# A scheduled kernel of a long convolution beside a gated feed-forward layer: the order of all engines from a per-operation table, b1 by one load and two column-tile transposes, 20 instead of 38 filler matmuls

## The chip, the cores and the metric

One core of one Trainium2 chip. The metric is the device time of one launch in microseconds (us), given as the median of several runs; the lowest and the highest run are in brackets. The profile's span is about 1.8 us shorter than the time of the same execution, because the time includes the start and end around the instructions. PE is TensorE's matmul, PEld its weight load, DVE is VectorE, ACT is ScalarE, POOL is GpSimd, SP is SyncE, which here mostly issues DMAs. A run counts as slow when it is over 1.5% above the fastest run of its kernel.

Ratios are the mean time of one kernel's fast runs over that of the kernel before in the same rounds on the same chip, so they are not quite the ratio of the medians that I quote.

## The reference

Shapes: sequence 2048, width D = 640, hidden width F = 1728, all bfloat16. Cut to what matters:

```python
x  = A_q                                   # 1 x 2048 x 640
xn = _layernorm(x)
# branch A: short convolution of k (4 taps), times v, then a convolution of length 2048 by FFT
k_shift = sum_t k_pad[:, t:t+S, :] * shift_k[:, 3-t]
kv = k_shift * v
y  = irfft(rfft(kv, 4096) * rfft(ssm_k, 4096))[:2048] + kv * ssm_D
s  = xn * y
# branch B: feed-forward layer with gelu, then silu as a gate
g  = silu(gelu(xn @ w1 + b1) @ w2 + b2)
# ... the output joins x, s and g
```

The kernel does the FFT as matmuls in stages, through scratch tensors in DRAM: a first stage for the filter's keys (scrK) and for kv (scrU), a small forward stage in tiles of 64 x 32, a product, an inverse in tiles of 32 x 64 (stored to scrC), and a last stage.

## The kernel before

The kernel is a list of operations. A planner (`Plan`) places each on an engine at a planned start, with a cost for each operation and a priority; the instructions are then emitted in the order of the planned starts. The psf and psa buffers are the kernel's PSUM buffers, where matmuls write: two psf of 512 columns and three psa of twice 512. The parts that the change and the argument touch:

```python
MODE_SWITCH = 0.095
# in Plan.schedule(): one pair of numbers for each kind of operation
for k, os in kinds.items():
    a, b = self.due[k]
    for i, o in enumerate(os):
        o.prio = -(a + (b - a) * i / max(1, len(os) - 1))
# ... list scheduling by the key (start, -prio, cost) ...

for i in range(38):                        # fillers, to raise TensorE's clock
    ps = Buf(pool=psf)
    op("PE", 0.22, lambda e, ps=ps: nc.tensor.matmul(out=ps.v[:, :], lhsT=hT_t[0][:, FT - 2, 0:P],
                          rhs=hT_t[0][:, FT - 2, :], start=True, stop=True), reads=[warm_b], writes=[ps], kind="warm")
# ... b1: memset, two loads on ScalarE's queue, one transpose, one copy
op("PE", 0.1, lambda e, ps=ps: nc.tensor.transpose(out=ps.v.bitcast(BF16)[:, 0:FT], in_=b1_r[:], identity=...))
op("DVE", 0.08, lambda e, ps=ps: nc.vector.tensor_copy(out=b1_f[:], in_=ps.v.bitcast(BF16)[:, 0:FT]))
# ... ffn1: one FF1 group of five matmuls of 512 columns into one of two psf banks, then gelu on ScalarE
for t in range(DT):
    nc.tensor.matmul(out=o, lhsT=w1_sb[:, t, ft*P:(ft+1)*P], rhs=xnT_b[c].v[:, :, t, :], start=(t == 0), stop=(t == DT-1))
# ... the small forward stage: eight matmuls in tiles of 64 x 32
def fwd(ps, src, z):
    for t in range(4):
        for r in range(2):
            nc.tensor.matmul(out=ps.v[t*32:t*32+32, r, 0:H], lhsT=F2m[r*Q:r*Q+Q, z*32:z*32+32],
                             rhs=src[r*Q:r*Q+Q, t, :], start=True, stop=True)
# ... middle(h, g): reload a group of the scratch into uin, forward stage, product, inverse, store to scrC
op("SP", 0.46, lambda e: nc.sync.dma_start(out=uin.v, in_=by_group(scrU[h], g)), ...)
```

Of the kernel before, what the change touches and what calls it, by code (L numbers as in the profile page):

```python
# [15 lines left out]
P = 128  # L16
# [50 lines left out]
TABLE_LOAD = 1.28  # L67
MODE_SWITCH = 0.095

class Plan:  # L70
# [42 lines left out]
    def schedule(self):  # L113
# [6 lines left out]
        for o in ops:  # L120
            for d in o.after:
                follow[d].append(o)
        kinds = {}
        for o in ops:
            kinds.setdefault(o.kind, []).append(o)
        for k, os in kinds.items():
            a, b = self.due[k]
            for i, o in enumerate(os):
                o.prio = -(a + (b - a) * i / max(1, len(os) - 1))
        for o in ops:  # L130
# [9 lines left out]
        while ready:  # L140
            best = None
            for o in ready:
                est, slots, ok = o.est, [], True
                for b in o.allocs:
                    cand = None
                    if b.pool.fifo and b.seq != b.pool.next:
                        ok = False
                        break
                    for s in b.pool.slots:
                        if any(s is c for c in slots) or any(u.done is None for h in s[1] for u in h.users):  # L150
                            continue
                        t = max([u.done for h in s[1] for u in h.users], default=0.0)
                        if cand is None or t < cand[0]:
                            cand = (t, s)
                    if cand is None:
                        ok = False
                        break
                    est = max(est, cand[0])
                    slots.append(cand[1])
                if not ok:  # L160
                    continue
                for e in o.engs:
                    t = max(est, free[e])
                    c = o.cost[e]
                    p = o.prio
                    if e == "ACT" and o.table is not None and o.table != table:
                        c += TABLE_LOAD
                        p -= self.due["switch"][0]
                    if e == "PE" and o.mode != mode:
                        c += MODE_SWITCH  # L170
                        p -= self.due["mode"][0]
                    if e != o.engs[0]:
                        wait, less = self.due["dve" if e == "DVE" else "pool"]
                        if max(est, free[o.engs[0]]) <= t + wait:
                            continue
                        p -= less
                    key = (t, -p, c)
                    if best is None or key < best[0]:
                        best = (key, o, e, t, c, slots)
# [33 lines left out]

DUE = {
    "b1": (-2658.69, -12.83), "cab0": (8557.17, 6667.77), "cab1": (-1486.18, -152.64), "cst0": (-305.42, 2707.06),
    "cst1": (-2821.97, -4792.38), "dve": (0.47, 30.2), "f1_0": (-871.05, 1734.66), "f1_1": (1301.71, 4641.74),
    "f1_2": (1114.17, 1732.61), "f1_3": (2717.88, 2832.21), "f1k0": (-526.64, -1917.59), "f1k1": (-45.43, 1009.63),
    "f1u0": (-4387.08, -5449.77), "f1u1": (-871.6, -2537.05), "f2_0": (-101.73, 568.69), "f2_1": (55.74, -1410.81),
    "f2_2": (2347.64, 580.24), "f2_3": (1367.74, 4253.7), "f2k0": (-4800.76, 938.43), "f2k1": (1474.47, -1695.6),
    "f2u0": (1087.17, -104.99), "f2u1": (-2201.6, -388.99), "fin0": (3005.36, 3026.91), "fin1": (4769.18, 4253.19),  # L220
    "first": (-4156.08, -3068.36), "gtab": (-2228.31, -2211.96), "halo1": (3569.33, 2410.81),
    "i10": (-236.08, -1811.7), "i11": (-1708.64, -1347.6), "i20": (2541.11, 1052.7), "i21": (2701.42, 3183.93),
    "kin0": (-593.69, 758.66), "kin1": (1951.88, -1170.69), "kt": (-677.48, -1093.47), "kv0": (-3727.38, -6497.24),
    "kv1": (818.93, -2911.39), "ln0": (-2934.3, -4187.58), "ln1": (-6791.26, -5326.47), "ln2": (1941.49, 937),
    "ln3": (896.12, -1662.13), "load1": (-2919.94, -4066.71), "load10": (1978.17, 919.81),
    "load11": (-2440.26, -3260.22), "load12": (4122.04, 8470.58), "load13": (7611.05, 3845.84),
    "load14": (3186.96, 908.54), "load15": (4188.27, 3598.3), "load16": (-1111.28, -467.99),
    "load17": (3134.69, 3049.36), "load18": (376.5, 3182.36), "load19": (1982.23, 428.93),
    "load2": (-5152.92, -6327.1), "load20": (5478.92, 7432.46), "load21": (-2345.4, 472.84),
    "load22": (-3453.91, -1273.89), "load23": (3030.08, 3625.43), "load24": (-2431.86, -3878.73),  # L230
    "load3": (-4653.66, -5026.1), "load4": (-4049.51, -2679.33), "load5": (-3127.18, -2370.67),
    "load6": (-1295.43, -2222.83), "load7": (-3086.77, -1734.57), "load8": (-486.48, 2101.2),
    "load9": (1995.94, 1552.87), "mode": (197.93, 0), "ones1": (-1676.37, -2952), "pool": (7.25, -13.8),
    "prod0": (69.2, -3781.34), "prod1": (2713.4, -508.43), "small": (-2624, 2474.77), "switch": (23.42, 0),
    "uin0": (-5019.36, -4445.98), "uin1": (-4066.58, -3058.07), "warm": (-9990.03, -8766.04),
    "wexp": (462.86, 314.56), "wtab": (-4840.89, -4511.51), "xt0": (-2587.15, -3103.92), "xt1": (191.84, -3623.5),
    "xt2": (1912.14, 2825.82), "xt3": (-3593.86, -3830.63),
}

@with_exitstack  # L240
def kernel(
# [47 lines left out]
    I1m = sb.tile([P, 3, Q], BF16, name="I1m")  # L289
    b1_r = sb.tile([FT, P], BF16, name="b1_r")  # L290
    b1_f = sb.tile([P, FT], F32, name="b1_f")
# [27 lines left out]

    plan = Plan(DUE)  # L320
    op = plan.op
# [6 lines left out]

    EV = (0.585, 0.735)
    psf = Pool(psf_t, fifo=False)  # L330
    psa = Pool(psa_t, fifo=False)
# [26 lines left out]
    op("DVE", 0.45, c0, writes=[bias_b, ones_b, mh_b], kind="first")  # L358
    op("DVE", 0.14, lambda e: nc.vector.memset(b1_r[:], 0.0), writes=[b1r_b], kind="first")

    warm_b = Buf()
    op("DVE", 0.2, lambda e: nc.vector.memset(hT_t[0][:, FT - 2, :], 0.0), writes=[warm_b], kind="first")
    for i in range(38):
        ps = Buf(pool=psf)
        op("PE", 0.22, lambda e, ps=ps: nc.tensor.matmul(out=ps.v[:, :], lhsT=hT_t[0][:, FT - 2, 0:P], rhs=hT_t[0][:, FT - 2, :],  # L365
                                                         start=True, stop=True),
           reads=[warm_b], writes=[ps], kind="warm")
# [8 lines left out]
    def load_rows(e):  # L376
        nc.scalar.dma_start(out=sk_row[0:1, :], in_=A_shift_k.rearrange("d j -> (d j)").rearrange("(o f) -> o f", o=1))
        nc.scalar.dma_start(out=dD_row[0:1, :], in_=A_ssm_D.rearrange("(o d) -> o d", o=1))
        nc.scalar.dma_start(out=b1_r[0:FT - 1, :], in_=B_b1[0:(FT - 1) * P].rearrange("(t p) -> t p", p=P))
        nc.scalar.dma_start(out=b1_r[FT - 1:FT, 0:FLAST], in_=B_b1[(FT - 1) * P:F].rearrange("(o p) -> o p", o=1))  # L380

    op("ACT", 1.0, load_rows, writes=[row_b, dD_b, b1r_b], kind="first", dma=1000)

# [11 lines left out]
    def load_w1(i):  # L395
        f0, f1 = W1B[i] * P, min(F, W1B[i + 1] * P)
        load(lambda e: nc.gpsimd.dma_start(out=w1_sb[:, :, f0:f1], in_=w1_v[:, :, f0:f1]), D * (f1 - f0) * 2,
             writes=[w1_b[i]], eng="POOL", cost=0.9)

# [57 lines left out]
    op("POOL", 0.4, w_iota, writes=[s16_b], kind="first")  # L457
    op("POOL", 0.9, lambda e: make_identity(nc, ident[:]), writes=[id_b], kind="first")
    op("POOL", 1.0, lambda e: nc.gpsimd.memset(k_all[0][0:1, 0:3, :], 0.0), writes=[halo_b[0]], kind="first")
# [14 lines left out]

    op("POOL", 0.5, lambda e: nc.gpsimd.memset(hT_t[0][FLAST:FLAST + 1, FT - 1, :], 1.0), writes=[], kind="first")

    for j in range(4):
# [11 lines left out]
    ps = Buf(pool=psf)  # L489
    op("PE", 0.1, lambda e, ps=ps: nc.tensor.transpose(out=ps.v.bitcast(BF16)[:, 0:FT], in_=b1_r[:], identity=ident[0:FT, 0:FT]),  # L490
       reads=[b1r_b, id_b], writes=[ps], kind="b1")
    op("DVE", 0.08, lambda e, ps=ps: nc.vector.tensor_copy(out=b1_f[:], in_=ps.v.bitcast(BF16)[:, 0:FT]), reads=[ps],
       writes=[b1_b], kind="b1")

# [125 lines left out]
    for t in range(DT):  # L620
# [10 lines left out]

        op("PE", 1.4, ktr, reads=[kf_b[t], id_b], writes=[ps], kind="kt")
        for h in range(2):
# [113 lines left out]

    op("DVE", 0.6, bits, writes=[small_b], kind="small")

# [5 lines left out]

    op("POOL", 2.2, phase, writes=[small_b], kind="small")

# [13 lines left out]

    op("POOL", 1.4, mats, writes=[small_b, F2_b, I1_b], kind="small")

# [144 lines left out]
```

## Time and profile before

| | before |
|---|---|
| time | 212.01 us (210.67 to 213.32, 3 runs) |
| span of the profiled execution | 208.5 us |
| first FF1 group starts | 19.66 us |
| last matmul ends | 203.70 us |
| tail after it | 4.8 us |

The lines are shown and read in the prediction. The way to read them is: split the span at the first FF1 group and at the last matmul; between the two, PE has almost no rest, so a change there must shorten PE's list of work, the switches between tile sizes, or PE's waits.

### The profile page before, as it was taken

The page shows a single profiled execution, that of the slowest core. Times are in us where ns is not written, and L with a number is a line of the kernel's source. Part 1 is how long each engine was busy: PE and PEld are TensorE (multiplying, and loading weights), DVE is VectorE, ACT ScalarE, POOL GpSimd, SP SyncE. Part 2 cuts the span into 40 slices and gives each one's busy share as a digit, 9 for nine tenths or more (in the row PEclk, how much of TensorE's full clock was granted, in tenths as well). Part 3 has the DMA queues.
Part 4 walks back from the last instruction along what each step waited for, and adds up shares of the span by engine and source line. Part 5 has one row for each costly group of instructions (what it writes and reads, how often), then busy time and mean ns, then how long its engine had stood idle before and what let it go on. Part 6 is the DMA issues. An engine that isn't in the chain of part 4 may idle for free.

```text
span 208.5 us, 5242 instructions
## 1 busy us (share of the span) xinstructions
PE 197.8 (95%) x2091; PEld 109.5 (53%) x2091; DVE 162.2 (78%) x301; ACT 148.2 (71%) x232; POOL 44.5 (21%) x67
## 2 busy tenths in 40 slices
PE   7997999989999999989999999999999899999990
PEld 2483446557676444334335666666643343667670
DVE  8879699999995543749899999562496676869993
ACT  2859879987787998769999776564579899830100
POOL 8992357400000001901201111001002021120000
PEclk9998899999999999999999999999999999999998
DMA  5999998993469899999964734896799963127994
GB/s 167 354 402 375 337 392 271 385 241 120 189 157 293 311 266 396 328 327 246 336 171 130 230 136 156 241 252 166 234 336 371 290 199 128 66 92 241 331 338 139
DMA packets 46137, 52.85 MB, mean 253 GB/s; under 512 B 14352, under 2 KB 35503, under 8 KB 46112
## 3 DMA queue, kind: packets, MB, share of 16 engines
q1 hardware_dynamic: 41920, 37.10, 58.0%
q0 software_dynamic: 4160, 15.40, 21.0%
q8 instruction: 16, 0.26, 0.5%
q14 instruction: 9, 0.07, 0.1%
q10 hardware_dynamic: 32, 0.01, 0.0%
HBM read 31.14 MB, written 18.35 MB: 237 GB/s over the span
## 4 chain that ended last, share of the span: by engine, by line
PE 66%; DVE 23%; DMA 6%; ACT 2%; issue 1%; SPq 0%; DVEq 0%
PE psf_105 L603 12%; PE psf_106 L603 11%; PE psf_106 L568 11%; PE psf_105 L568 9%; DVE GAB L689 5%; DVE stats L500 4%; DMA kv_90<-scrU_66 4%; DVE GAB L696 3%; DMA kv_90<-scrU_65 3%; PE psf_105 L365 3%; PE psf_106 L365 2%; PE psa_109 L851 2%; PE psa_108 L851 2%; PE psa_107 L816 2%; DVE xreg L520 2%; DVE xreg L878 2%
## 5 line engine op out<-in xcount | busy, mean ns | idle before, releaser
L568 PEld LDWEIGHTS <-w_sb 128*128 128x128 bf16 x280 | 25.1, 98 | 33.2 <-issue 9.0
L568 PE MATMUL psf_106<-hx_93,w_sb 128*128 128x512 bf16 x105 | 27.2, 391 | 0.8 <-ACT hx_93 L324 0.8
L568 PE MATMUL psf_105<-hx_93,w_sb 128*128 128x512 bf16 x105 | 26.2, 380 | 1.1 <-ACT hx_93 L573 1.1
L603 PEld LDWEIGHTS <-hx_93 128*128 128x128 bf16 x224 | 21.5, 98 | 9.4 <-issue 1.1
L603 PEld LDWEIGHTS <-hx_94 128*128 128x128 bf16 x224 | 21.7, 98 | 8.9 <-issue 0.5
L696 DVE TENSOR_TENSOR GAB<-GAB 128x1280 bf16<-128x1280 bf16 x24 | 19.6, 817 | 0.0
L603 PE MATMUL psf_105<-w_sb,hx_93 128*128 128x320 bf16 x112 | 16.6, 299 | 0.0
L603 PE MATMUL psf_106<-w_sb,hx_93 128*128 128x320 bf16 x112 | 16.6, 299 | 0.0
L603 PE MATMUL psf_105<-w_sb,hx_94 128*128 128x320 bf16 x112 | 16.6, 299 | 0.0
L603 PE MATMUL psf_106<-w_sb,hx_94 128*128 128x320 bf16 x112 | 16.5, 299 | 0.0
L858 POOL DMA_DIRECT2D scrC_67<-kv_90 x8 | 6.0, 754 | 49.0 <-ACT kv_90 L324 29.5
L500 DVE BATCH_NORM_STATS2 stats<-xreg 128x6 f32<-128x320 bf16 x32 | 13.7, 471 | 0.3 <-DMA xreg<-in_A_q_dram 0.2
L858 POOL DMA_DIRECT2D scrC_68<-kv_90 x8 | 6.0, 752 | 37.4 <-DVE kv_90 L324 15.2
L689 DVE TENSOR_TENSOR GAB<-kv_91,w_exp 128x1280 bf16<-128x1280 bf16 x16 | 13.0, 821 | 0.1
L689 DVE TENSOR_TENSOR GAB<-kv_90,w_exp 128x1280 bf16<-128x1280 bf16 x16 | 12.9, 818 | 0.0
L324 ACT CAST kv_90<-psa_108 128x640 bf16<-128x640 f32 x18 | 12.6, 701 | 0.4 <-PE psa_108 L851 0.3
L573 ACT ACTIVATE hx_93<-psf_105,b_f 128x512 bf16<-128x512 f32 (+1 forms) x14 | 9.9, 706 | 3.1 <-PE psf_105 L568 3.1
L816 PEld LDWEIGHTS <-F2m 64*32 64x32 bf16 x512 | 5.2, 89 | 12.9 <-issue 11.7
L573 ACT ACTIVATE hx_93<-psf_106,b_f 128x512 bf16<-128x512 f32 x14 | 9.8, 704 | 2.4 <-PE psf_106 L568 2.3
L324 ACT CAST kv_90<-psa_109 128x640 bf16<-128x640 f32 x15 | 10.4, 695 | 1.0 <-PE psa_108 L816 0.4
L418 POOL DMA_DIRECT2D kv_91<-in_A_v_dram x2 | 1.8, 915 | 43.2 <-ACT kk_96 L324 38.8
L573 ACT ACTIVATE hx_94<-psf_106,b_f 128x512 bf16<-128x512 f32 x14 | 9.7, 696 | 1.6 <-PE psf_106 L568 1.0
(191 smaller groups left out, 451.4 us busy)
## 6 DMA issues: line engine op xcount, KB each, us to landing
hx_94<-in_A_ssm_k_dram SPq DMA_DIRECT2D x5, 512.0 KB, 6.7
kv_90<-scrU_65 SPq DMA_DIRECT2D x8, 320.0 KB, 5.1
scrC_67<-kv_90 POOLq DMA_DIRECT2D x8, 320.0 KB, 5.5
kv_90<-scrU_66 SPq DMA_DIRECT2D x8, 320.0 KB, 4.5
kv_91<-scrC_67 SPq DMA_DIRECT2D x8, 320.0 KB, 5.0
scrC_68<-kv_90 POOLq DMA_DIRECT2D x8, 320.0 KB, 3.7
out_dram<-xreg SPq DMA_DIRECT2D x16, 160.0 KB, 4.5
kv_91<-scrC_68 SPq DMA_DIRECT2D x8, 320.0 KB, 4.8
```

The costliest lines, as they stand in the source:

```text
L324: (nc.scalar.copy if e == "ACT" else nc.vector.tensor_copy)(out=out_, in_=in_)
L365: op("PE", 0.22, lambda e, ps=ps: nc.tensor.matmul(out=ps.v[:, :], lhsT=hT_t[0][:, FT - 2, 0:P], rhs=hT_t[0][:, FT - 2, :], start=True, st ...
L500: nc.vector.bn_stats(out=stats[:, c, j, h, :], in_=x_b[c].v[:, j, h * H:(h + 1) * H])
L520: nc.vector.tensor_scalar(out=o, in0=i, scalar1=rstd[:, c, j:j + 1], scalar2=nmr[:, c, j:j + 1], op0=ALU.mult, op1=ALU.add)
L568: nc.tensor.matmul(out=o, lhsT=w1_sb[:, t, ft * P:(ft + 1) * P], rhs=xnT_b[c].v[:, :, t, :], start=(t == 0), stop=(t == DT - 1))
L573: op("ACT", 0.575, lambda e: nc.scalar.activation(out=hT_b[c].v[0:M, ft, :], in_=ps.v[0:M, :], func=ACT.Gelu_apprx_tanh, bias=b1_f[0:M, ft ...
L603: nc.tensor.matmul(out=ps.v[:, 0:H], lhsT=hT_b[c].v[0:M, ft, q * P:(q + 1) * P], rhs=w2_sb[0:M, ft, hs], start=(ft == 0), stop=(ft == FT - 1))
L689: nc.vector.tensor_tensor(out=out_, in0=k_all[h][:, r + 3 - j:r + 3 - j + KR, :], in1=w_exp[:, j, None, hs].to_broadcast([P, KR, H]), op=A ...
L696: op("DVE", 0.735, lambda e, t=t: nc.vector.tensor_tensor(out=a.v, in0=a.v, in1=t.v, op=ALU.add), reads=[t], writes=[a], kind="kv%d" % h)
L816: nc.tensor.matmul(out=ps.v[t * 32:t * 32 + 32, r, 0:H], lhsT=F2m[r * Q:r * Q + Q, z * 32:z * 32 + 32], rhs=src[r * Q:r * Q + Q, t, :], st ...
L851: nc.tensor.matmul(out=pc[t // 2].v[r * Q:r * Q + Q, t % 2, 0:H], lhsT=I1m[t * 32:t * 32 + 32, w, :], rhs=pr[a].v[t * 32:t * 32 + 32, 2 * ...
L858: op("POOL", 0.85, lambda e: nc.gpsimd.dma_start(out=by_group(scrC[h], g), in_=cs.v), reads=[cs], writes=[scrC_b[h][g]], kind="cst%d" % h, ...
```

## The change

Its intent: let a search set a priority (and, for some, the engine) for every single operation, rather than two numbers for each kind; give the planner better costs for TensorE's mode switches; take the load of b1 and the first block of w1 out of the way; and issue fewer fillers. The arithmetic stays the same.

```diff
-MODE_SWITCH = 0.095
+MODE_SWITCH = (0.093, 0.115, 0.137)
-        for k, os in kinds.items():
-            a, b = self.due[k]
-            for i, o in enumerate(os):
-                o.prio = -(a + (b - a) * i / max(1, len(os) - 1))
+            o.prio, o.force = self.due["ops"][o.i]
 ...
+                    if o.force >= 0 and len(o.engs) > 1 and e != o.engs[o.force]:
+                        continue
 ...
-DUE = { "b1": (-2658.69, -12.83), "cab0": ... }          # two numbers for each kind
+ORDER = { ..., "ops": ((-2.6, -1), (-7.24, -1), ...) }   # one pair for each operation
-    for i in range(38):
+    for i in range(20):
-        nc.scalar.dma_start(out=b1_r[0:FT - 1, :], ...)
-        nc.scalar.dma_start(out=b1_r[FT - 1:FT, 0:FLAST], ...)
+    op("SP", 0.46, lambda e: nc.sync.dma_start(out=b1_r[:], in_=B_b1.rearrange("(t p) -> t p", p=Q)), ...)
-        load(lambda e: nc.gpsimd.dma_start(out=w1_sb[:, :, f0:f1], ...
+        dma = nc.sync.dma_start if i == 0 else nc.gpsimd.dma_start
+    def b1_t(e, ps=ps):
+        for u in range(2):
+            nc.tensor.transpose(out=ps.v.bitcast(BF16)[half(u), 0:F // Q], in_=b1_r[:], ...)
+    def b1_copy(e, ps=ps):
+        for u in range(2):
+            nc.vector.tensor_copy(out=b1_f[half(u), 0:FT - u], in_=ps.v.bitcast(BF16)[half(u), u:F // Q:2])
```

Some costs told to the planner were corrected as well, and one memset moved from POOL to DVE.

## The prediction

> **What bounds the kernel now.** I read the page first, then busy time by stage, then the PE timeline, then ACT's timeline ahead of the first large matmuls. The page, then four stretches of the windows view (columns: us, then busy us and instructions of PE, PEld, DVE, ACT, POOL; granted clock; DMA share; GB/s):
>
> ```profile
> PE 197.8 (95%) x2091; PEld 109.5 (53%) x2091; DVE 162.2 (78%) x301; ACT 148.2 (71%) x232; POOL 44.5 (21%) x67
> ...
> 0.00:11.78 11.78, 10.27 (x40) 4.18 (x40) 8.76 (x30) 7.18 (x4) 10.90 (x25) 1.00 0.80 278
> 11.78:19.66 7.88, 6.54 (x78) 4.95 (x78) 7.64 (x22) 5.38 (x8) 5.42 (x8) 0.95 1.02 384
> 19.66:203.70 184.04, 180.95 (x1976) 100.35 (x1975) 144.24 (x247) 135.25 (x220) 28.18 (x35) 0.99 0.80 249
> 203.70:208.50 4.80, 0.00 (x1) 0.00 (x0) 1.52 (x4) 0.44 (x1) 0.00 (x0) 0.81 0.45 141
> ```
>
> The reader should see three stages: an opening until 19.66 us, where the first matmul group of the feed-forward part (L568, "FF1") starts; a body of 184.0 us in which PE hardly stops; and a tail of 4.8 us (silu, multiply, add, store) after the last matmul. DVE and ACT have slack over the whole body. So PE's own list of work sets the body, and what sets the opening is to be found.
>
> The PE timeline (start us, busy us, line, output<-inputs, count) shows what the body is made of:
>
> ```profile
> 4.89 0.58 PE L365 MATMUL psf_105<-hx_93 128*128 128x512 bf16 x1
> 5.31 0.38 PE L365 MATMUL psf_106<-hx_93 128*128 128x512 bf16 x1
> 5.53 0.38 PE L365 MATMUL psf_105<-hx_93 128*128 128x512 bf16 x1
> ...
> 19.66 2.29 PE L568 MATMUL psf_106<-hx_93,w_sb 128*128 128x512 bf16 x5 [0.76 <-ACT hx_93 L324]
> ...
> 84.56 1.25 PE L568 MATMUL psf_105<-hx_93,w_sb 128*128 128x512 bf16 x5
> 85.75 0.33 PE L816 MATMUL psa_107<-kv_90,F2m 64*32 64x320 bf16 x8
> 86.01 1.25 PE L568 MATMUL psf_106<-hx_93,w_sb 128*128 128x512 bf16 x5
> 87.10 1.24 PE L568 MATMUL psf_105<-hx_93,w_sb 128*128 128x512 bf16 x5
> 88.17 1.24 PE L568 MATMUL psf_106<-hx_93,w_sb 128*128 128x512 bf16 x5
> ```
>
> Read the differences of starts, not the durations, which overlap. An FF1 group of five costs 88.17-87.10 = 1.07 to 1.08 us if another follows. If the small tiles of L816 follow, it costs 85.75-84.56 = 1.19, and the eight tiles (0.136 us more for each further eight) take 0.26. One excursion of PE into the small tiles and back thus costs about 0.11+0.12 = 0.23 us beyond its work. The inverse groups (L851) show the same: 0.68 us against 0.54 of streaming. Also, the filler matmuls go from 0.42 to 0.22 us apart at 5.31, and the first FF1 group ran at half speed (2.08 us from start to the next matmul).
>
> Last, ACT before the first FF1 group:
>
> ```profile
> 2.20 1.28 ACT L467 ACT_TABLE_LOAD   x1 [2.20 <-DVE hx_93 L362]
> 5.76 2.00 ACT L467 ACTIVATE WB<-w_sb,sin_bias 128x2048 bf16<-128x2048 int32 x1 [2.27 <-DVE w_sb L465]
> 7.66 1.99 ACT L469 ACTIVATE w_sb<-w_sb,turn 128x2048 f32<-128x2048 int32 x1
> 9.68 2.00 ACT L471 ACTIVATE WA<-w_sb,cos_bias 128x2048 bf16<-128x2048 f32 x1
> 14.02 1.93 ACT L324 COPY kv_91<-psa_108 128x1024 bf16<-128x1024 bf16 x2 [2.33 <-PE psa_108 L626]
> 15.83 0.71 ACT L324 COPY hx_93<-psf_106 128x640 bf16<-128x640 bf16 x1
> 16.41 0.73 ACT L324 COPY hx_93<-psf_105 128x640 bf16<-128x640 bf16 x1
> 17.40 1.01 ACT L324 COPY kv_91<-psa_109 128x1024 bf16<-128x1024 bf16 x1 [0.26 <-DVE kv_91 L324]
> 18.31 0.70 ACT L324 COPY hx_93<-psf_106 128x640 bf16<-128x640 bf16 x1
> 18.89 0.71 ACT L324 COPY hx_93<-psf_105 128x640 bf16<-128x640 bf16 x1
> ```
>
> FF1 needs the four copies of transposed activations (hx_93). The last starts at 18.89 and FF1 at 19.66. ACT idled 2.33 us ahead of 14.02, waiting for PE's first key transposes; these started only at 11.78, behind 38 filler matmuls, though the first key load, issued at 2.13, takes 5.6 us to land (about 7.7). That idle time is what a better order can take out.
>
> **What the Trainium skill says.** "TensorE: Matmul & The Clock Gate", Part 1, says the array's clock is halved by default and freed after a window of about 3.4 us of activity, and that an idle window halves it again. The trace agrees: half speed to 5.3 us, and again at 19.66 after the loose opening. "TensorEngine Tiling (Array Packing)", Key Properties: "Changing tiling mode (not just tile) drains the TensorE". The 0.23 us per excursion agree. "ScalarE: Activation LUTs", What ACT_TABLE_LOAD costs, gives 1283 ns a load (here 1.28) plus a drain of 1380 ns; here the next activation starts 1.30 us after the last load before FF1 began, so I charge 1.28. "DMA: Bandwidth & Descriptors", Issuing engines are not separate DMA queues, says that another issuing engine saves issue time only. The trace fits: DMA share is about 1.0 from 6 to 30 us, so spreading the loads changes their order, not their rate.
>
> **The change part by part.** The arithmetic is the same. Most of the diff is a number per operation in place of a number pair per kind; I take the result from the emitted instruction order, not from the table, and take no time from the planner's own cost model.
>
> *Fillers and b1.* 38 fillers become 20 (18 x 0.22 = 3.9 us of PE). They lie before 11.78, and PE then waits for other things, so this is worth nothing by itself. b1's second transpose and copy cost about 0.06 us of PE and 0.17 us of DVE; the memset, one DMA issue and 0.27 us of ACT's issue time go. Net: 0.
>
> *PE's list.* From the key transposes on, I multiply counts by the intervals above: FF1 56 x 1.08 = 60.5; second layer (L603) 32 x 1.91 = 61.1; first-stage transforms (L669) 64 x 0.27 = 17.4; small forward tiles 64 x 0.136 = 8.7; inverse 16 x 0.54 = 8.7; last stage 16 x 0.54 = 8.7; transposes and row expansion 5 x 0.99 + 4 x 0.28 + 4 x 0.55 = 8.3. Sum 173.4, the same in both. Switches are what differs: the old order enters the forward tiles from full-size matmuls 27 times and the inverse 16 times, with 6 steps straight from inverse to forward; the new one 21, 16 and 5. At 0.09 into a mode, 0.115 out of forward and 0.137 out of inverse, that is 10.0 against 8.6 us. **Saved: 1.4 us.**
>
> *Work moved into the opening.* Before its first FF1 group the old order does 3 key transposes, 2 of 4 row expansions and 2 transforms. The new one does 4, 4 and 0. That is +0.99 +1.10 -0.54 = **1.5 us** less for the body.
>
> *Start of FF1.* The new ACT order is: load a table, two row expansions, the Abs, a second table load, the two Sin, one normalization, two more expansions, two hx copies, one key copy, two hx copies. The Abs needs DVE's product and mask (2.22 + 0.27 + 1.18 from about 1.3, so 5.0). Then 2.0 + 1.28 + 2.0 + 2.0 = 12.3; 0.6 for the normalization; 2 x 0.58, 2 x 0.58, 0.95, 2 x 0.58 (intervals from ACT's rows) = 17.4. FF1 follows at about 17.5 if nothing on this chain waits. DVE's part (statistics of six chunks and the norms, about 1.0 and 0.36 each) ends near 15.6 and feeds the last two copies in time; PE's second and third key transposes wait for the ACT expansions at about 13.6 and fit too. I allow 0.5 us for slips: 18.0 against 19.66, **1.7 us**. One more table load is inside this.
>
> *Waits in the body.* 184.0 us of body against 177.5 by the sum over its list leaves 6.5 us. About 1.3 of it is the half-speed clock at 19.66, some 4 us are six waits of 0.3 to 0.95 us (ahead of 39.5, 42.5, 56.7, 79.2, 93.6, 162.9: ACT and DVE evictions and two scratch reloads), and the rest is small. The new order is again near the limit of DVE in 40 to 60 us (DVE busy 10.0 of 10 before), so I expect most of these to be replaced by others, and take **1.0 us**.
>
> Sum: 1.4 + 1.5 + 1.7 + 1.0 = 5.6 us. Span 208.5 - 5.6 = 202.9; the same ratio, 0.973, on the 212.0 median gives **206.3 us**. The tail is unchanged, since a second-layer group is still last.
>
> **The rivals.** First, new waits take the saving back. For: the second weight block used by FF1's fifth group now goes out on GpSimd's queue only after the phase instructions, at about 16.6, and these loads took 9 to 10 us, while the fifth group is due at about 24 to 25; the forward tiles now come in threes and fill all three psa buffers. Against: fewer bytes are in flight then. If it holds, 2 to 3 us are lost: 208.5 to 209. Second, the opening is bound by something I put off the path, such as the row load or the granted clock falling at the transposes instead of at FF1: then the start gains nothing, 208. Third, the half-speed window is avoided and most waits vanish: 203.5. Fourth, the body is bound by DVE rather than PE; against it, PE is busy 180.95 of 184.04 us. That rival would give 211 to 212.
>
> **Range and chances.** The switches and the moved work, 2.9 us, are close to certain; start and waits are plus or minus 2 each. The line for 2% is 207.8, 1.5 us above my figure, so: range 203.6 to 209.6, faster 0.66, within 2% 0.32, slower 0.02.
>
> **What would show it.** First FF1 at 17.5 to 18.5; ACT without an idle stretch of over 1 us between 5 and 17 us; last matmul near 198; the tail still 4.8; 37 excursions from full-size matmuls against 43; body waits of 5 to 6 us in all. A first FF1 after 19.5, or new waits over 7 us in the body (look at the fifth FF1 group and at the first read of the scratch), would make the prediction wrong.

## The result, and the profile after

| | before | after |
|---|---|---|
| time, median (lowest to highest) | 211.34 us (210.65 to 213.32, 4 runs) | 202.76 us (202.37 to 204.67, 4 runs) |
| ratio of fast runs, 95% interval | | 0.9598 (0.9505 to 0.969) |
| span of the profile | 208.5 | 200.6 |
| first FF1 group | 19.66 | 18.63 |
| last matmul ends | 203.70 | 196.20 |
| tail | 4.80 | 4.40 |

The predicted 206.3 us was 3.5 us too high, and 202.76 lies 0.8 us below the range. The direction was right. Of the 3.5 us, 2.3 are in the spans (202.9 predicted, 200.6 measured). The other 1.2 come from the conversion: the profile before is of an execution of 210.28 us, but its ratio was put on the median of 212.01. The changed kernel by stage, in the windows view (columns as in the prediction: us, busy us and instructions of PE, PEld, DVE, ACT, POOL; granted clock; DMA share; GB/s):

```profile
0.00:10.80 10.80, 7.96 (x22) 2.21 (x22) 9.68 (x27) 8.16 (x7) 5.62 (x19) 1.00 0.84 282
10.80:18.63 7.83, 7.21 (x95) 6.08 (x94) 7.55 (x31) 6.96 (x9) 4.50 (x7) 1.00 0.93 367
18.63:196.20 177.57, 176.10 (x1960) 99.68 (x1959) 145.41 (x244) 132.75 (x216) 31.39 (x40) 1.00 0.85 261
196.20:200.60 4.40, 0.00 (x1) 0.00 (x0) 1.52 (x4) 0.44 (x1) 0.00 (x0) 1.00 0.35 112
```

The body fell from 184.04 to 177.57 us, so 6.5 of the 7.9 us of the span are there. In the second stage the clock is 1.00 where it was 0.95, and ACT is busy for 6.96 of 7.83 us where it was busy for 5.38 of 7.88. (The 1.00 of the first stage is no reading: the clock record begins only with the first full-speed window. The fillers stand 0.42 us apart, as at half speed, until about 10.2 us here and until 5.3 before.) The difference of the spans then splits by the prediction's own method. PE's work from the first FF1 group on is 167.5 us before and 166.0 after (the sum of the prediction less what each does ahead of that group); the switches are 10.0 and 8.6. What is left of the body after these two is waiting: 184.04 - 167.5 - 10.0 = 6.5 us before, 177.57 - 166.0 - 8.6 = 2.95 after.

| term | predicted, us | from the two profiles, us |
|---|---|---|
| start of FF1 | 1.7 | 1.0 |
| work moved into the opening | 1.5 | 1.5 |
| mode switches | 1.4 | 1.4 |
| waits in the body | 1.0 | 3.6 |
| tail | 0 | 0.4 |
| sum | 5.6 | 7.9 |

Two of these terms, moved work and switches, are counted from the emitted order with durations of the trace. Of the others the start and the tail are read directly, and the waits are the remainder. PE's waits view shows the same without the sum. Its rows for the body, before and then after (us in total, times, longest us):

```profile
PE psf_105 L568 <- ACT hx_93 L573: 1.1, 2, 0.7
PE psa_107 L851 <- DVE kk_96 L324: 0.6, 1, 0.6
PE psa_109 L816 <- DMA kv_90<-scrU_66: 0.6, 1, 0.6
PE psa_108 L669 <- DVE kv_90 L699: 0.5, 1, 0.5
PE psa_107 L816 <- DMA kv_90<-scrU_65: 0.2, 1, 0.2
```

```profile
PE psa_107 L926 <- DMA kv_90<-scrU_65: 1.1, 1, 1.1
PE psf_105 L713 <- ACT sl_103 L717: 0.2, 1, 0.2
```

The opening on ACT (start us, busy us, line, output<-inputs; in brackets how long ACT had idled, and what ended it):

```profile
12.30 0.91 ACT L633 ACTIVATE xreg<-xreg,nmr,rstd 128x640 bf16<-128x640 bf16 x1
13.11 0.67 ACT L424 CAST w_exp<-psa_109 128x640 bf16<-128x640 f32 x1
13.69 0.69 ACT L424 CAST w_exp<-psa_107 128x640 bf16<-128x640 f32 x1
14.27 0.70 ACT L424 COPY hx_93<-psf_105 128x640 bf16<-128x640 bf16 x1
14.85 0.71 ACT L424 COPY hx_93<-psf_106 128x640 bf16<-128x640 bf16 x1
16.37 1.01 ACT L424 COPY kv_91<-psa_109 128x1024 bf16<-128x1024 bf16 x1 [0.81 <-DVE kv_91 L424]
17.28 0.70 ACT L424 COPY hx_93<-psf_105 128x640 bf16<-128x640 bf16 x1
17.87 0.71 ACT L424 COPY hx_93<-psf_106 128x640 bf16<-128x640 bf16 x1
```

The chain is the predicted one up to 14.85. Then ACT idles 0.81 us ahead of a copy of transposed keys, until a DVE copy from the same psa buffer ends, and the last copy that FF1 needs ends at 18.58 where I had 17.4.

The one large wait of the body, in the chain of waits between 80 and 97 us (start us, us, what):

```profile
84.33 11.46 DMA kv_90<-scrU_65
95.78 0.04 issue
95.83 0.33 PE psa_107 L926 x8
```

and the DMA issues around it, first on SP's queue, then on POOL's:

```profile
84.33 6.46 SPq L935 DMA_DIRECT2D kv_90<-scrU_65  x3
```

```profile
81.71 0.90 POOL L514 DMA_DIRECT2D kv_91<-in_A_k_dram  x1
...
83.91 0.91 POOL L514 DMA_DIRECT2D kv_91<-in_A_k_dram  x1
84.81 0.89 POOL L521 DMA_DIRECT2D kv_91<-in_A_v_dram  x1
```

A small forward group at 95.83 waits for a reload of the scratch (kv_90<-scrU_65) that was issued at 84.33 and landed 11.46 us later. Together with that reload, POOL has issued the loads of k and v for the second half of the channels. PE stands still for 1.12 us there, the largest of the 2.95.

### The profile page after: what moved, and what is told of

Same layout as the page of the kernel before. It is cut to its first block, busy times and chain, and to the rows that moved or that the text cites. A ratio compares the mean times of both kernels' runs of the same rounds, so it can differ in the third digit from the quotient of the medians.

```text
span 200.6 us, 5212 instructions
## 1 busy us (share of the span) xinstructions
PE 191.3 (95%) x2074; PEld 108.0 (54%) x2074; DVE 164.2 (82%) x303; ACT 148.3 (74%) x232; POOL 41.5 (21%) x65
## 4 chain that ended last, share of the span: by engine, by line
PE 76%; ACT 8%; DVE 7%; DMA 6%; issue 1%; DVEq 0%
PE psf_105 L713 14%; PE psf_106 L713 14%; PE psf_106 L678 14%; PE psf_105 L678 13%; DMA kv_90<-scrU_65 6%; PE psa_107 L779 3%; PE psa_108 L779 3%; PE psa_109 L779 2%; DVE xreg L988 2%; PE psa_107 L926 2%; PE psa_109 L926 2%; PE psa_108 L926 2%; PE psa_107 L961 2%; PE psa_108 L961 1%; PE psa_109 L961 1%
## 5 line engine op out<-in xcount | busy, mean ns | idle before, releaser
L713 PEld LDWEIGHTS <-hx_93 128*128 128x128 bf16 x224 | 21.3, 98 | 10.2 <-issue 2.2
L713 PEld LDWEIGHTS <-hx_94 128*128 128x128 bf16 x224 | 21.4, 98 | 9.4 <-issue 1.0
L678 PE MATMUL psf_106<-hx_94,w_sb 128*128 128x512 bf16 x70 | 17.5, 381 | 0.0
L678 PE MATMUL psf_105<-hx_94,w_sb 128*128 128x512 bf16 x70 | 17.5, 380 | 0.0
L678 PE MATMUL psf_105<-hx_93,w_sb 128*128 128x512 bf16 x70 | 17.4, 379 | 0.0
L678 PE MATMUL psf_106<-hx_93,w_sb 128*128 128x512 bf16 x70 | 17.4, 379 | 0.0
L799 DVE TENSOR_TENSOR GAB<-kv_91,w_exp 128x1280 bf16<-128x1280 bf16 x16 | 12.5, 816 | 1.4 <-DMA kv_91<-in_A_k_dram 1.4
L799 DVE TENSOR_TENSOR GAB<-kv_90,w_exp 128x1280 bf16<-128x1280 bf16 x16 | 12.5, 813 | 0.0
L424 ACT CAST kv_90<-psa_108 128x640 bf16<-128x640 f32 x17 | 11.9, 698 | 0.8 <-PE psa_108 L961 0.6
L683 ACT ACTIVATE hx_94<-psf_105,b_f 128x512 bf16<-128x512 f32 x14 | 9.8, 698 | 2.1 <-PE psf_105 L678 2.0
L683 ACT ACTIVATE hx_93<-psf_106,b_f 128x512 bf16<-128x512 f32 (+1 forms) x14 | 9.8, 700 | 2.0 <-PE psf_106 L678 1.8
L683 ACT ACTIVATE hx_93<-psf_105,b_f 128x512 bf16<-128x512 f32 (+1 forms) x14 | 9.9, 704 | 1.7 <-PE psf_105 L678 1.5
```

The lines of the kernel that those rows point to most:

```text
L424: (nc.scalar.copy if e == "ACT" else nc.vector.tensor_copy)(out=out_, in_=in_)
L678: nc.tensor.matmul(out=o, lhsT=w1_sb[:, t, ft * P:(ft + 1) * P], rhs=xnT_b[c].v[:, :, t, :], start=(t == 0), stop=(t == DT - 1))
L683: op("ACT", 0.575, lambda e: nc.scalar.activation(out=hT_b[c].v[0:M, ft, :], in_=ps.v[0:M, :], func=ACT.Gelu_apprx_tanh, bias=b1_f[0:M, ft ...
L713: nc.tensor.matmul(out=ps.v[:, 0:H], lhsT=hT_b[c].v[0:M, ft, q * P:(q + 1) * P], rhs=w2_sb[0:M, ft, hs], start=(ft == 0), stop=(ft == FT - 1))
L799: nc.vector.tensor_tensor(out=out_, in0=k_all[h][:, r + 3 - j:r + 3 - j + KR, :], in1=w_exp[:, j, None, hs].to_broadcast([P, KR, H]), op=A ...
```

## The experiments

Besides whole-order exchanges, each experiment edits only what an operation issues, or moves a few operations in the emitted list; the planner's result stays as it was, so all else keeps its order. "Waits" below is always the same remainder: first FF1 to last matmul, less the listed work and switches. It comes from the one profiled execution of each kernel.

**1. Fewer fillers in the old order.**

```diff
-        op("PE", 0.22, lambda e, ps=ps: nc.tensor.matmul(
+        op("PE", 0.22, lambda e, ps=ps, i=i: None if i >= 20 else nc.tensor.matmul(
```

> The kernel before with 20 filler matmuls in place of 38, nothing else. The prediction put this at 0 us. Rival: in the kernel before DVE idled 1.8 us behind the b1 transpose, which stood behind the fillers, and the first key load had landed at about 7.7 us while the key transposes started at 11.78, so 18 fillers fewer start the opening earlier: 1.0 to 2.0 us faster (209.5 to 210.5 where the kernel before is at 211.3). A third way: the idle PE loses its clock earlier and the key transposes run at half speed: up to 1 us slower.

Measured: 209.06 us (207.73 to 210.67), ratio 0.9879 (0.9813 to 0.9946), so about 2.5 us faster (1.2%). The PE timeline of this kernel:

```profile
1.51 7.42 PE L365 MATMUL psf<-hx 128*128 128x512 bf16 x20 [1.51 <-DVE hx L362]
8.86 0.18 PE L490 MATMUL psf<-ident,b_r 14*128 14x14 bf16 x1
...
18.34 2.29 PE L568 MATMUL psf<-hx,w_sb 128*128 128x512 bf16 x5 [0.76 <-ACT hx L324]
```

The kernel before, same view for PE, and DVE's row that waited for it:

```profile
11.67 0.18 PE L490 MATMUL psf_105<-ident,b_r 14*128 14x14 bf16 x1
```

```profile
11.88 0.17 DVE L492 CAST b_f<-psf_105 128x14 f32<-128x14 bf16 x1 [1.79 <-PE psf_105 L490]
```

The fillers are on the path in the old order: b1's transpose stands behind the last of them, DVE idles 1.79 us for it with the normalization queued behind, and the first FF1 group starts 1.3 us later than with 20. "Worth nothing by itself" was wrong. The gain does not hold in every execution: the profiled one, the slowest of the four at 210.67, had the early start and 8.1 us of waits.

**2. The changed kernel without eight of its fillers**, those that stand behind the first key transposes.

```diff
+  None if i in (1, 3, 6, 7, 8, 12, 16, 17) else nc.tensor.matmul(
```

> The changed kernel without the 8 fillers that stand between the first key transposes and the first activation transposes. If these fillers are what holds the clock through the opening (the kernel before showed 3.4 us at half speed from 18.9 us on, the changed one none), the half-speed stretch returns at about 14 to 20 us and costs 1 to 2 us (203.8 to 204.8). If the fillers are of no use, the time stays within 0.4 us of 202.8.

Measured: 204.77 us (203.29 to 206.65), ratio 0.9674 (0.9599 to 0.9749). Its profile is of a slow run, so only what it shows by itself is used. The windows view in the opening, and PE's longest wait:

```profile
11.00:13.00 2.00, 1.03 (x17) 0.98 (x16) 1.91 (x10) 2.00 (x2) 0.60 (x1) 1.00 1.02 391
13.00:16.40 3.40, 3.40 (x33) 3.40 (x33) 2.90 (x15) 2.56 (x5) 1.70 (x5) 0.50 1.06 425
```

```profile
PE psa L926 <- DMA kv<-scrU: 3.4, 1, 3.4
```

Without these fillers PE rests for about 1 us at 12 us and the clock is halved from 13.0 to 16.4; FF1 starts at 19.00, 0.37 us later. No other profile of the new opening, nine with these fillers, has a half-speed window there. But the fillers are not always needed: of the three fast runs without them, the one of 205.68 us has a mean granted clock of 1.000 and the one of 203.29 has 0.996, and a window of 3.4 us would give 0.992 or less. So the fillers lower the chance of losing the clock at most, and the clock does not explain the 205.68. The larger part of the loss in this execution is elsewhere: the wait for the scratch reload grew from 1.12 to 3.4 us, and a second half-speed window followed it at 98.4. That pointed to experiment 8.

**3 and 4. One kernel's opening with the other's body.** The opening keeps its kernel's own order up to the first FF1 group; the remaining operations follow the other kernel's order and engines.

```diff
-        for o in self.schedule():
+        own = self.schedule()          # up to the first FF1 group; then the order of the other kernel, where legal
+        for o in own[:cut] + by_other(own[cut:]):
             o.fn(o.eng)
```

> The changed kernel up to its first FF1 group, and from there on all remaining operations in the relative order and on the engines of the kernel before (27 and 16 entries into the small tiles again). If the body's order is worth 1.4 us of switches and 2.3 us of waits, this is 3.7 us slower than the changed kernel: about 206.5. If the gain lies in the opening alone (earlier start, work moved, clock kept), it stays at 203 to 204.5. If the body's order does it all, 209 or more.

Measured: 214.33 us (209.4 to 215.77); only one of four runs is fast, so there is no ratio. In that run (209.4), FF1 started at 18.62, and the waits were 8.5 us.

> The kernel before up to its first FF1 group, and from there on the remaining operations in the relative order and on the engines of the changed kernel (21 and 16 entries). If the body's order is worth 3.7 us: about 207.6 where the kernel before is at 211.3. If the gain lies in the opening alone: 210 to 211.5. If the body's order does it all: 204 or less.

Measured: 217.23 us (215.7 to 218.67), ratio 1.0286 (1.0213 to 1.0359), with waits of 14.3 us and three half-speed windows. PE's waits view (us in total, times, longest us):

```profile
PE psf L796 <- ACT hx L801: 3.7, 2, 3.5
PE psa L1044 <- DMA kv<-scrU: 2.2, 1, 2.2
```

In the first exchange the one fast run fits only my last branch, 209 or more; in the second all of my figures were too low. Up to 6.8 us of its 14.3 are the half-speed windows (13.7 us at half speed), so the second exchange does not measure the order alone. Neither half of the new order shows a gain of its own next to a half that it was not made with: waits of 1.7 to 3.5 us appear where loads and evictions come at other times. So the gain cannot be added up from halves, and these runs cannot say how much each half brings.

**5. All the small parts in the old order**: 20 fillers, the new b1 path, the first w1 block on SP's queue.

```diff
-    for i in range(38): ...                        -> 20 issued, in the same slots
-    b1: memset, two loads on ScalarE's queue, ...  -> one load on SyncE's queue, two transposes, two copies
-    nc.gpsimd.dma_start(out=w1_sb[:, :, f0:f1] ...  -> nc.sync.dma_start for block 0
```

> The kernel before in its own order, with all of the small parts: 20 fillers, b1 by one load and two column-tile transposes, the first block of w1 on SyncE's queue. The kernel before with 20 fillers alone ran in 209.06 us against 210.96. My theory (b1 and the w1 block are worth nothing by themselves): 208 to 210 us, ratio 0.985 to 0.995, first FF1 within 0.5 us of the 18.34 of the filler cut alone. Rival (the b1 path held the opening's critical path, since VectorE idled 1.79 us for it): first FF1 before 17.6 and 206 to 208 us. What is left of the 8.6 us to the changed kernel is then the order's.

Measured: 211.62 us (211.19 to 212.01), ratio 1.0033 (0.9945 to 1.0121). FF1 started at 18.34, exactly as with the filler cut alone, and yet nothing is left at the end: the waits were 9.5 us. My time was too low; that b1 and w1 do not move the start was right. In this run the old order turned the earlier start into waits; the interval leaves room for a gain of 1.2 us.

**6 and 7. The old small parts in the new order.** The first try had a fault of mine: I put the memset of b1's rows behind their loads.

```diff
+        nc.vector.memset(b1_r[:], 0.0)             # run 6: in the constants on VectorE, behind the loads
+        nc.scalar.dma_start(out=b1_r[0:FT - 1, :], ...)  # as before, and one transpose and one copy
-        dma = nc.sync.dma_start if i == 0 else nc.gpsimd.dma_start
+        dma = nc.gpsimd.dma_start
# run 7: the memset stands first in load_rows, ahead of the loads
```

> The changed kernel in its own order with 20 fillers, but b1 loaded and transposed in the old way (a memset, two loads, one transpose, one copy) and the first block of w1 back on GpSimd's queue. My theory (both are worth nothing by themselves, the order carries the gain): 202.4 to 204 us, first FF1 18.4 to 19.0. Rival (the w1 block comes late from GpSimd's queue, or the b1 loads on ScalarE's queue delay its first table load): first FF1 1 us later or more, 204.5 us or more.

Measured: 205.42 us (204.85 to 207.69), ratio 0.9766 (0.9667 to 0.9865). DVE's first rows there:

```profile
4.26 0.11 DVE L460 MEMSET b_r<- 14x64 uint32 x1 [2.61 <-DMA b_r<-in_B_b_dram]
4.30 2.25 DVE L568 TENSOR_TENSOR w_sb<-kk 128x2048 int32<-128x2048 f32 x1
```

The memset waited for the load, DVE's table operations began 2.7 us late (4.30 against 1.58), and FF1 began 2.4 us late, at 21.02. (It also zeroed b1, and the result still passed the comparison.) The run says nothing of the b1 path, but it shows by accident that a delay at the start of DVE's list reaches FF1 almost whole: 2.4 of 2.7 us.

> The changed kernel in its own order and with 20 fillers, b1 in the old way and the first w1 block on GpSimd's queue, as in the run before it, but with the memset of b1's rows ahead of their loads: in that run it stood behind them, VectorE waited 2.61 us for the load before its first table operation, and all of the opening came that much later (first FF1 21.02 us). Theory: without that wait the old parts cost nothing: first FF1 at 18.4 to 19.1 us, 202.3 to 203.5 us. Rival (the second load of the table or the w1 block itself were late): first FF1 still after 20 us, 204.5 us or more.

Measured: 202.6 us (202.33 to 204.51), ratio 0.9592 (0.952 to 0.9665), FF1 at 18.68. In the new order, the b1 path and the queue of the first w1 block are worth nothing. With experiment 5, what is left for the difference of the two kernels is the order, the place of the fillers in it included; the interval of experiment 5 leaves about 1 us for the small parts in the old order.

**8. Two loads later.** In the changed kernel, the second half of k and v of the second head group goes behind the second store of the scratch.

```diff
+MOVES = ((("load23", 0), ("cst0", 1)), (("load24", 0), ("load23", 0)))
+        for key, behind in MOVES: ...              # takes the operation out and puts it behind the other
```

> The changed kernel with two loads moved alone: the second half of k and v of the second head group, issued at 81.7 and 84.8 us in the profile of the changed kernel, go behind the second store of the scratch (91.7 us). Theory: their 1.3 MB share the memory system with the reload of the scratch issued at 84.33 us, for which TensorE waited 1.19 us at 93.5 us (3.45 us in the run without eight fillers); without them the wait falls below 0.5 us and the time to 201 to 202.3 us, with less spread between executions. Rival: the reload waits for the stores of the scratch or for its place on SyncE's queue; then the wait stays at 1 us or more and the time within 202.4 to 204.7 us.

Measured: 201.0 us (200.99 to 201.63), ratio 0.9544 (0.9476 to 0.9612). POOL's issues and PE at the place of the wait:

```profile
92.48 0.90 POOL L528 DMA_DIRECT2D kv<-in_A_k_dram  x1
93.37 0.89 POOL L535 DMA_DIRECT2D kv<-in_A_v_dram  x1
```

```profile
92.35 2.33 PE L692 MATMUL psf<-hx,w_sb 128*128 128x512 bf16 x10
94.61 0.47 PE L940 MATMUL psa<-kv,F2m 64*32 64x320 bf16 x16
```

The reload is issued at the same moment (84.31 us). By its semaphore it has landed at 91.44, 7.1 us after its issue instead of 11.46, and the forward group follows FF1 without a wait. (The next reload but one, issued at 90.4, lands after 3.6 us instead of 8.7.) The rival, that the reload waits for stores or for its place in the queue, is out. Waits: 1.6 us. This version beats both kernels in every run, and its spread is 0.6 us.

**9. An earlier FF1.** In the changed kernel, the key copy at 16.37 us goes behind the last two activation copies, one key transpose behind the last activation transposes, one behind the first FF1 group, and one DVE copy behind a small operation.

```diff
+MOVES = ((("kt", 0), ("xt0", 6)), (("kt", 7), ("xt0", 7)), (("kt", 2), ("small", 3)), (("kt", 10), ("f1_0", 0)))
```

> The changed kernel with four operations of the opening moved alone: one ScalarE copy of transposed keys goes behind the last two activation copies, one key transpose behind the last activation transposes, one behind the first FF1 group, and one VectorE copy behind a small operation. Theory: the first FF1 group at 18.63 us stood behind the last activation copy (ended 18.58), which ScalarE reached late for that key copy at 16.37 to 17.38 us; with the moves it starts at 17.4 to 18.0 us and the kernel takes 201.6 to 202.3 us. Rival: the key transposes put off return the gain as a wait of the first small-transform groups, and the time stays at 202.4 to 204 us, or half speed comes back in the opening and it rises.

Measured: 203.77 us (203.71 to 206.94, the highest of them slow), ratio 0.9667 (0.9585 to 0.9749), so about 1 us slower than the changed kernel. PE:

```profile
17.49 1.24 PE L694 MATMUL psf<-hx,w_sb 128*128 128x512 bf16 x5
18.57 1.17 PE L752 MATMUL psa<-ident,hx 128*128 128x128 bf16 x16
...
21.56 1.17 PE L752 MATMUL psa<-ident,hx 128*128 128x128 bf16 x16 [0.20 <-DVE kv L440]
23.24 1.24 PE L694 MATMUL psf<-hx,w_sb 128*128 128x512 bf16 x5 [0.52 <-ACT hx L699]
```

The rival holds. FF1 starts at 17.49 as my prediction had wanted, but 1.0 us of key transposes is now in the body, and new waits for DVE and ACT cost 1.5 us more than in the changed kernel. So this way of starting FF1 earlier is not worth its own size; others were not tried.

**10 and 11. The mode switch by itself.** In the middle of each of the 64 groups of eight small tiles, one matmul of one column into an unused column: of full size in run 10, with small tiles in run 11 (the control).

```diff
     for t in range(4):
+        if t == 2:   # run 10
+            nc.tensor.matmul(out=ps.v[:, 0, H:H + 1], lhsT=ident[:], rhs=src[:, 0, 0:1], start=True, stop=True)
+        if t == 2:   # run 11
+            nc.tensor.matmul(out=ps.v[0:32, 0, H:H + 1], lhsT=F2m[0:Q, z*32:z*32+32], rhs=src[0:Q, 0, 0:1], ...)
```

> The changed kernel with one full-size matmul of one column (128 x 128 weights, into an unused PSUM column) in the middle of each of the 64 groups of eight small-tile matmuls. It adds 64 excursions into full size and back; at the 0.093 + 0.115 us that I took from the trace of the kernel before, 13.3 us of switching, and at most 3 us for the matmuls themselves: 215 to 220 us. Rival: the switch is only the ordinary pipeline gap of a new group and costs nothing by itself; then under 208 us, and the same as the run with a small-tile matmul in that place.

> The control: in the same 64 places one matmul of one column with small tiles (64 x 32 weights), which changes no size on the way. Theory: 64 x about 0.02 us, so 203.5 to 206 us. The difference to the run with full-size matmuls, divided by 64, is the cost of one excursion (my figure: 0.21 us).

Measured: 218.83 us (218.76 to 219.01), ratio 1.0343, with full size; 204.71 us (202.62 to 206.13), ratio 0.9594, with small tiles, of which two runs are slow and the fast ones are 202.62 and 203.48. One reading of PE with the full-size matmuls:

```profile
69.05 0.18 PE L926 MATMUL psa<-kin,ident 128*128 128x1 bf16 x1
69.16 0.33 PE L928 MATMUL psa<-kin,F2m 64*32 64x320 bf16 x8
69.42 0.18 PE L926 MATMUL psa<-kin,ident 128*128 128x1 bf16 x1
```

From one full-size matmul to the next is 0.37 us, of which eight tiles are 0.136, so an excursion into full size and back costs 0.23 us with its own matmul. Against the mean of the control's fast runs, (218.83 - 203.05) / 64 = 0.25 us each. The full-size run has no wait for the reload near 95 us, though, and the two bodies without that wait, of this run and of experiment 8, differ by (193.97 - 176.22) / 64 = 0.28 us. So an excursion with its own matmul is 0.23 to 0.28 us, and my figure of 0.21 plus a little for the matmul stands at its lower end. Six excursions fewer in the changed kernel are about 1.4 us.

**12. The changed kernel once more**, unaltered.

> The changed kernel unaltered once more, for its spread: I expect 202.3 to 204.7 us, with a wait for the reload of the scratch near 93 us between 1 and 3.5 us. If it comes out at 201.0 to 201.6 us as the version with the two late loads did, that version is not better.

Measured: 202.62 us (202.22 to 205.51), ratio 0.9568 (0.9498 to 0.9637); PE waited 1.3 us for the reload, which took 11.6 us from issue to landing. None of its runs comes down to the 201.63 that was the highest of experiment 8.

**13. The half-speed window alone.** The old order with 38 fillers and 13 more, of 192 columns, in the two gaps ahead of its first FF1 group.

```diff
+    def keep_warm(n):
+        for _ in range(n):
+            nc.tensor.matmul(out=psa_t[2][:, 0, H:512], lhsT=hT_t[0][:, FT - 2, 0:P], rhs=hT_t[0][:, FT - 2, 0:512 - H], ...)
+    keep_warm(5)    # ahead of the first first-stage transform
+    keep_warm(8)    # ahead of the first FF1 group
```

> The kernel before in its own order with 13 further fillers of 192 columns in the two gaps in which TensorE waited ahead of its first FF1 group (17.6 to 18.15 and 18.75 to 19.66 us), into an unused part of PSUM. Theory: in the kernel before, half speed came from 18.9 to 22.4 us because TensorE idled in these gaps; with the fillers the half-speed window goes from the opening and with it the wait of 1.01 us at the first FF1 group (and 0.26 after it), so the waits after FF1 fall from 6.4 to about 5.1 us and the kernel to 209 to 210.5 us. Rival: the window comes all the same, somewhat later, or the fillers hold FF1 up; then 210.5 us or more, with the waits at 6 us or more.

Measured: 212.65 us (212.33 to 214.2), ratio 1.0087 (1.0016 to 1.0159). PE:

```profile
12.30 0.18 PE L496 MATMUL psf<-ident,b_r 14*128 14x14 bf16 x1
...
19.40 0.57 PE L336 MATMUL psa<-hx 128*128 128x192 bf16 x5 [1.14 <-ACT kv L324]
...
21.30 0.82 PE L336 MATMUL psa<-hx 128*128 128x192 bf16 x8 [0.78 <-ACT io L324]
21.95 1.24 PE L576 MATMUL psf<-hx,w_sb 128*128 128x512 bf16 x5
23.03 0.30 PE L679 MATMUL psa<-kv,WA 128*128 128x320 bf16 x1
```

Both halves of my expectation came in part. In the profiled run the half-speed window is gone, and the first FF1 group takes 1.08 us to the next matmul instead of 2.08. But the fillers themselves waited for a buffer (1.14 and 0.78 us) and held FF1 up, to 21.95. So the time cannot be used; the waits can. They are 6.1 us, with the window's 1.3 out of them and others larger, above all one of 1.6 us near a scratch reload at 161 us. The window explains 1.3 us of the kernel before at most; without it, the old order still waits for 6 us. That the 13 fillers keep the clock up is not shown by this run: PE had longer gaps here (1.14 and 0.78 us) than the one of 0.52 us ahead of 18.9 us in the kernel before, and the clock stayed. Nor did it stay in every run: the other three have mean clocks of 0.978 to 0.981, which is 8 to 9 us at half speed, more than the tail of 5.0 us can hold. So the time of this run cannot say what the window is worth, for this reason too.

A second thing shows here. In this execution the clock rose at 6.6 us and not at 5.3, so the same 38 fillers ended 0.63 us later and b1's transpose with them (12.30 against 11.67). A part of the old order's spread may come in that way; two executions do not show it.

## Why the prediction was right or wrong

*PE's list and the moved work.* Right: 1.5 us, and the sum of work and switches fits the body to within its waits in both kernels.

*Switches.* Right: 37 excursions from full-size matmuls against 43, and experiments 8, 10 and 11 give 0.23 to 0.28 us each.

*"Fillers and b1 ... Net: 0."* The b1 path is worth nothing (experiments 5 and 7). "PE then waits for other things" failed for the fillers: b1's transpose stood behind them, and DVE behind it, and cutting 18 moved FF1 by 1.3 us (experiment 1). In the sum that movement belongs to the start of FF1, where I had counted it a second way, so the sum was not off by it.

*Start of FF1, 1.7 us.* Mis-sized: 1.0 us. The chain was right up to 14.85; ACT's idle 0.81 us ahead of one key copy was missing. In the one way tried, experiment 9, the missing part was worth nothing: the key transposes that were put off, 1.0 us, came back in the body, and waits with them. (The 1.30 us that the prediction quotes for a table load is that of the load at 21.21 us, which stands ahead of FF1's first gelu and behind FF1's first matmul.)

*Waits in the body, 1.0 us.* This is the step that failed. The prediction's sentence was: "I expect most of these to be replaced by others". They were not: 6.5 us of waits became 2.95, a term of 3.6 where 1.0 was predicted. That is 2.6 us too little; with -0.7 at the start and +0.4 in the tail it makes the 2.3 us by which the sum of spans fell short. The reason given, that the new order is again near the limit of DVE from 40 to 60 us, was half true and did not matter: DVE is busy for 18.79 of these 20 us (20.00 before), yet PE is busy for 19.80 (18.88 before). Nor had DVE "slack over the whole body" before, as the prediction's first part says. Of the 3.6, about 1.3 is the half-speed window, which I had named among the waits of the kernel before and then did not take off, although the new opening has fillers where the old one had gaps. That the fillers are what keeps it away is not shown (two runs of experiment 2 kept the clock without eight of them). The profiled run of experiment 13 shows that with a full clock the waits at the first FF1 groups are gone. The rest, about 2.3 us, goes with the order as a whole; experiments 3 and 4 do not let it be given to the order of the body alone. The profiles of the old order have 6.1 to 9.5 us of waits (before and experiments 1, 5, 13), those of the new one 2.95 to 3.5 (after and experiments 6, 7, 12), 1.6 without the collision of loads. The new order can be worse: 4.4 us with the moves of experiment 9, 6.9 in the slow run of experiment 2. My reading, which no run tests, is that a priority for each operation can place each load and eviction, so that waits need not move from one place to another.

*The rivals.* The third, "the half-speed window is avoided and most waits vanish: 203.5", was the nearest; I gave it too little. The first, new waits that take the saving back, is what happened in experiments 3, 4, 5 and 9, but not in the change. The fifth FF1 group, which it feared, did not wait; a reload of the scratch near 95 us did, for 1.12 us. DVE as the bound is out: PE was busy 176.10 of 177.57 us.

*What stays open.* What exactly halves the clock, and what keeps it up in the kernel before with more fillers, is not settled. Which single moves in the new body remove the old waits (ahead of 39.5, 42.5, 56.7, 79.2, 93.0 and 162.9 us) was not isolated; the whole-order exchanges show that they cannot be taken one half at a time. And why an early start in the old order was kept in some executions of experiment 1 and lost in all of experiment 5 was not found: the waits that took it differed from place to place.

## What to carry to other kernels

Where one engine is busy for 95% of the span, count its work and its waits apart, and ask of every wait whether the new order has a reason for it; a new order tuned as a whole may simply have fewer. Filler matmuls are instructions in a queue: look at what stands behind them, and where the clock fell after a gap, a few may be worth a trial there; here their use was not shown. When a reload of a few hundred KB is late, look at what bulk load was issued just before on any queue, and move that one if its user comes much later: two moved loads took another 1.6 us off here.

## What the Trainium skill lacked or had wrong

- "TensorE: Matmul & The Clock Gate", HAM oscillation, has the abstract rule "no PE-idle gaps >~3.4µs". (Its section on a second failure mode speaks of micro-idles too, without a figure.) In the bodies of the 15 profiles the clock was halved after all four gaps of 2.23 us or more (2.23, 2.40, 3.37, 3.50) and after none up to 2.09. In the openings, where transposes and one-row matmuls take most of PE's time, it was halved after shorter ones, of 0.52 us ahead of 18.9 us in the kernel before and of 0.97 us ahead of 13.0 us in experiment 2, and not after one of 1.14 us in experiment 13. So there a gap of 0.5 to 1 us can be enough, and is no sure trigger. All these windows but one lasted 3.4 us, the length that the page gives; the one at 20.9 us in experiment 4 lasted twice as long.
- The same page, Part 1, says that the number of cold matmuls varies from run to run, and the trace agrees (the clock rose at 5.3 and at 6.6 us with the same fillers). It does not say that the work behind the fillers inherits this: 0.63 us at b1's transpose.
- "TensorEngine Tiling (Array Packing)", Key Properties, says that a change of mode drains TensorE, without a figure: 0.23 to 0.28 us for an excursion and back here.
- "ScalarE: Activation LUTs", What ACT_TABLE_LOAD costs, adds a drain of about 1380 ns to each load. In the changed kernel the next activation starts 1.30 us after the start of the load at 7.20 us, which took 1.28; no further drain is seen.
- "DMA: Bandwidth & Descriptors", Issuing engines are not separate DMA queues, says that transfers from all issuers interleave; it has no figure for what that does to a small one: the reload of 320 KB that PE waits for near 95 us took 11.5 us to land in the changed kernel beside the bulk loads, and 7.1 us in experiment 8 with two of them moved.
